# Plain float32 scores in two row halves, plain float32 diagonal products, one pool of eight banks, and new planner costs

## The chip, the core and the metric

The kernel runs on one core of a Trainium2 chip. The metric is the time of one execution in microseconds on the device. The core's engines work side by side and meet through semaphores: PE (TensorE, the matmuls; PEld is its weight load), DVE (VectorE), ACT (ScalarE), POOL (GpSimd) and SP (SyncE, which issues most DMAs). PE writes to PSUM, which has eight banks; POOL works on SBUF alone.

## The reference, cut to what matters

A gated recurrent attention (mLSTM) over 4 batches, 8 heads, 768 positions and 40 channels a head is followed by a token mix of rank 32 and an MLP from 320 to 1280 to 320 channels, all in float32.

```python
for t in range(S):                                    # attention, per batch and head
    m_new = max(f[t] + m, i[t])
    C = exp(f[t] + m - m_new) * C + exp(i[t] - m_new) * outer(v[t], k[t])
    n = exp(f[t] + m - m_new) * n + exp(i[t] - m_new) * k[t]
    m = m_new
    y[t] = sigmoid(o[t]) * (C @ q[t]) / max(abs(n @ q[t]), 1)
x  = y, heads side by side                            # [B, 768, 320]
u  = x + (x^T @ U @ V)^T                              # mix over the positions
out = u + relu(u @ w1) @ w2
```

## The kernel before

The recurrence is computed in chunks of 128 positions. Each batch has two halves (`hf`) of three chunks; in each half the heads form groups of 3, 3 and 2, so a batch has 16 units of one head and one half. For a unit:
- `scores` (line 775) multiplies k and q of each chunk on PE, 3 matmuls of 128 columns into one PSUM bank (`ps`).
- `decay_scan` (760) builds the products of the forget gates, `dm`, by a scan on DVE. Its input is a row of gates spread over 128 partitions: a PE matmul (`decay`, 757, in PSUM) for the first 11 units, a DMA (`load_decay`, 759, tile `fd` in SBUF) for the others.
- `weigh` (777) multiplies scores and decays on DVE into `wt`.
- `pv` (799) is the diagonal product of `wt` and the values on PE.

For each group come `kv` (695) and `inter` (808), the sums of keys and values for the state C and the part that the state gives; `state`, `norm`, `out_norm` and `gate` finish x.

Two precisions exist side by side. Of 64 units the first 21 multiply q and k as plain float32 with 40 rows (`SPLIT_FROM`). The others split them into a rounded part (`qk_high`, 743, a cast on ACT) and remainders (`qk_low`, 745, on POOL or DVE), stacked to 120 rows in the tile `sk`, so that one matmul in the faster float32r format makes the sum. In the same way the first 19 units multiply `wt` and v as plain float32 (`BF_FROM`, by whole groups); the others cut both into three bfloat16 parts (`thirds`, 609: `part1` and `part2` on ACT, `rest1` and `part3` on POOL or DVE) and add six products of parts, 18 matmuls a unit.

The MLP of one half (`mlp`, 914) runs 10 steps: `up` (935), 8 matmuls of 384 columns of high and low weight parts; `relu_high` (942, ACT) and `relu_low` (944, DVE); `down` (964), 9 matmuls of 320 columns. The weights arrive as 64-bit words, and 22 pieces are converted by ACT (518) and three DVE steps each (519, 521, 523) before `w_high` (567) and `w_low` (568) make the parts.

The order on every engine is made when the program is built: `Plan.schedule` (178) picks for each engine, by its costs and by due times (`pri`), the operation that can start first; the queues then run in that order. Where PE would be empty, `keep_busy` (145) puts in matmuls of zeros (`zeros`), called fillers below. `BANKS` and `SHARE` (95, 96) give three banks to `down` and five to all else. MLP steps of batch b lie among the attention of batch b + 1. The program adds its work in this order: gates, weights, attention of batch 0, then for each batch the attention of the next, two mixes and two MLPs.

Of the kernel before, what the change touches and what calls it, by code (L numbers as in the profile page):

```python
# [20 lines left out]
P = 128  # L21
# [21 lines left out]
STACK = 3 * D  # L43

PARTS = ((0, 2), (0, 1), (0, 0), (1, 1), (1, 0), (2, 0))
SPLIT_FROM = 21
FB_FROM = 11
BF_FROM = 18
# [19 lines left out]
WIDE_DMA = 630.0  # L68

# [12 lines left out]
    "qk": (3, [STACK, 2, HS], F32),  # L82
    "sk": (1, [STACK, 2, HS], F32R),
# [11 lines left out]
BANKS = {"m2": 3, "ps": 5}  # L95
SHARE = {"st": ("ps", 5), "at": ("ps", 5), "m1": ("ps", 5)}
# [5 lines left out]
class Plan:  # L102


    def __init__(self, slots):
        self.slots = {tag: [[tile, 0.0, None, tag] for tile in tiles] for tag, tiles in slots.items()}
        self.ops, self.at, self.busy = [], {}, defaultdict(float)
# [8 lines left out]
    def op(self, kind, pri, eng, cost, fn, r=(), w=(), new=(), stream="", load=1.0):  # L116
# [26 lines left out]
        self.ops.append((pri, eng, cost, fn, sorted(deps), after, new, owners, load))  # L143

# [33 lines left out]
    def schedule(self, filler, ENGINE):  # L178
# [8 lines left out]
        free, ring, dma = defaultdict(lambda: BEGIN), 0.0, 0.0  # L187
        ready = {n: 0.0 for n in range(len(ops)) if waits[n] == 0}
        left = dict(self.uses)
        while ready:  # L190
            picks = {}
            for n, est in ready.items():
                pri, engs, cost, fn, deps, after, new, owners, load = ops[n]
                s = est
                for key, tag in new:
                    group, most = SHARE.get(tag, (tag, len(self.slots.get(tag, ()))))
                    open_at = [sl[1] for sl in self.slots[group] if sl[2] is None]
                    s = max(s, min(open_at)) if open_at and self.held[tag] < most else float("inf")
                if s == float("inf"):
                    continue  # L200
                if isinstance(engs, str):
                    picks.setdefault(engs, []).append((max(s, free[engs]), pri, n))
                else:
                    done = [max(s, free[e]) + c for e, c in zip(engs, cost)]
                    e = engs[done.index(min(done))]
                    picks.setdefault(e, []).append((max(s, free[e]), pri + (ALT_PRI if e == "dve" else 0), n))
# [54 lines left out]
def mlstm_mixer_kernel(  # L261
# [91 lines left out]
    def gates():  # L353
# [29 lines left out]
        for hf in range(2):  # L383
# [11 lines left out]
            def start(hf=hf, m=m, fs=fs):  # L395
# [6 lines left out]
                "gate_max", pre, "dve", 530,  # L402
# [11 lines left out]
            def ends(bst=bst, fs=fs):  # L414
# [17 lines left out]
                "gate_w", pr, "dve", 469,  # L432
# [7 lines left out]
                "gate_g", pr, "dve", 469,  # L440
# [177 lines left out]
    def attention(b, base):  # L618
# [5 lines left out]
        def at(n):  # L624
            return base + 88.6 * n / span
# [6 lines left out]
        def group(j, n):  # L632
# [62 lines left out]
            p.op("kv", at(n - 0.5), "pe", 215 * nk, kvmm, r=[(kt, "k"), kv2], w=[kk], new=[(kk, "st")], stream="att", load=0.95)  # L695
# [33 lines left out]
            for hh in range(nh):  # L729
                bh = b * NHEAD + h0 + hh  # L730
                u = n + hh
                kqk, ksk, kdm, kw, kfb, ks = [(s, b, j, hh) for s in ("qk", "sk", "dm", "wt", "fb", "sp")]
                split = u + 16 * b >= SPLIT_FROM
                rows = STACK if split else D

                def load_qk(kqk=kqk, hh=hh, rows=rows):
                    nc.sync.dma_start(
                        out=T[kqk][0:rows].rearrange("p n s -> p (n s)"), in_=qk[b, h0 + hh, hf, 0:rows],
                    )

                p.op("load_qk", at(u) - 7, "sp", dma(rows * 2 * HS * 4), load_qk, w=[kqk], new=[(kqk, "qk")])
                if split:
                    p.op("qk_high", at(u - 1), "act", 733, lambda kqk=kqk, ksk=ksk: nc.scalar.copy(T[ksk], T[kqk]),  # L743
                         r=[kqk], w=[(ksk, 0), (ksk, 1)], new=[(ksk, "sk")])
                    for n2, lo in ((0, slice(0, D)), (1, slice(64, 64 + D))):
                        p.op("qk_low", at(u - 1), *both(HS), lambda e, n2=n2, lo=lo, kqk=kqk, ksk=ksk: e.tensor_sub(  # L746
                            T[ksk][lo, n2, :], T[kqk][lo, n2, :], f32(T[ksk][lo, n2, :])), r=[kqk], w=[(ksk, n2)])
# [8 lines left out]
                if u + 16 * b < FB_FROM:  # L756
                    p.op("decay", at(u), "pe", 165, fbmm, r=[("fhl", hf), ("fh", hf), ("idents",)], w=[kfb], new=[(kfb, "at")], load=0.5)
                else:
# [5 lines left out]
                    r=[kfb, ("idents",)], w=[kdm], new=[(kdm, "dm")],  # L764
                )

                def scmm(ks=ks, ksk=ksk, kqk=kqk, split=split):
                    for c in range(3):
                        cs = slice(c * P, (c + 1) * P)
                        if split:  # L770
                            mm(T[ks][:, cs], T[ksk][:, 1, cs], T[ksk][:, 0, cs])
                        else:
                            mm(T[ks][:, cs], T[kqk][0:D, 1, cs], T[kqk][0:D, 0, cs])

                p.op("scores", at(u), "pe", 330 if split else 640, scmm, r=[(ksk, 0), (ksk, 1)] if split else [kqk], w=[ks], new=[(ks, "at")],
                     load=0.45 if split else 0.31)
# [7 lines left out]
                def pvmm(hh=hh, kw=kw, kpb=kpb):  # L784
# [15 lines left out]
                    "pv", at(u + 1), "pe", 460 if fine else 640, pvmm,  # L800
                    r=[(k, i) for k in (kpb, kvb) for i in range(3)] if fine else [kw, (kt, "v")], w=[(kn, hh)],
                    new=[(kn, "st")] if hh == 0 else [], stream="att", load=0.65 if fine else 0.32,
# [6 lines left out]
                "inter", pf, "pe", 215 * (3 - c0), immm,  # L809
# [280 lines left out]
```

## Time and profile before

| | us |
|---|---|
| median of 3 runs | 486.63 (485.9 to 488.29) |
| span of the profiled execution | 484.6 |
| PE busy | 433.1 (89%) |
| DVE busy | 358.4 (74%) |
| POOL busy | 242.1 (50%) |
| ACT busy | 207.8 (43%) |
| mean granted TensorE clock | 0.875 |

The span is the time from the first to the last instruction; the run's time lies about 2 us over it. A busy PE is one that has a matmul in flight, at whichever clock. The granted clock is 1.0 at 2.4 GHz and 0.5 at 1.2 GHz, so a share between is a mean over both. A float32 matmul appears in the trace as two records, a float32r or bfloat16 one as one. Matmuls overlap, so the time that a block takes is read from its start to the start of the block behind it.

### The profile page before, as it was taken

Reading aid. Unit: us, or ns where it says so; the run is one execution under the profiler, and the core shown is the slowest. Engines: PE = TensorE matmul, PEld = TensorE weight load, DVE = VectorE, ACT = ScalarE, POOL = GpSimd, SP = SyncE. Lnnn points to the kernel's source line nnn. Section 1 sums busy time; section 2 is a strip of 40 time slices with the busy share of each in tenths; the row PEclk is TensorE's granted clock in tenths of the full one; section 3 lists DMA queues with packets and bytes.
Section 4 is the critical chain, followed back from the end, with each engine's and each line's share of the span. In section 5 each row is a group of like instructions: output and inputs, shape, how many; then the busy total and the mean of one; then the engine's idle time right before and its main releaser. Section 6 shows DMA issues by size and latency. Waiting matters only on the chain.

```text
span 484.6 us, 8703 instructions
## 1 busy us (share of the span) xinstructions
PE 433.1 (89%) x3175; PEld 398.1 (82%) x3175; DVE 358.4 (74%) x611; ACT 207.8 (43%) x485; POOL 242.1 (50%) x229
## 2 busy tenths in 40 slices
PE   6999999996888689889879798798888999999996
PEld 4788888985777678889768688797887889999996
DVE  6655565769999999984999998968999995322132
ACT  4411120545454655563545764544556553311120
POOL 2323244569777798730776956625768660000000
PEclk9555555579789899899989999999899999999999
DMA  8325344777475464551565656722647301010011
GB/s 247 114 87 177 94 133 137 229 201 186 134 238 171 115 177 126 157 162 48 137 169 167 167 139 170 204 81 89 182 125 180 90 3 41 1 42 0 1 42 41
DMA packets 31642, 60.58 MB, mean 125 GB/s; under 512 B 4160, under 2 KB 19776, under 8 KB 31600
## 3 DMA queue, kind: packets, MB, share of 16 engines
q1 hardware_dynamic: 31407, 59.63, 43.4%
q8 instruction: 25, 0.41, 0.4%
q10 hardware_dynamic: 192, 0.40, 0.2%
q14 instruction: 18, 0.14, 0.1%
HBM read 55.79 MB, written 4.23 MB: 124 GB/s over the span
## 4 chain that ended last, share of the span: by engine, by line
PE 51%; DVE 25%; POOL 11%; issue 9%; DMA 2%; ACT 1%; POOLq 0%; DVEq 0%; SPq 0%; ACTq 0%
PE ps L284 34%; PE m L284 17%; POOL sk L746 5%; DVE dm L762 4%; DVE cv L521 2%; DMA q<-in_q 2%; DVE C L701 2%; DVE sk L746 2%; DVE h L944 2%; DVE cv L523 2%; DVE wt L777 2%; POOL v L662 1%; POOL h L866 1%; DVE wt L612 1%; DVE pb L614 1%
## 5 line engine op out<-in xcount | busy, mean ns | idle before, releaser
L284 PE MATMUL ps<-ut,w1h 128*128 128x384 f32 x400 | 125.7, 352 | 3.6 <-DVE h L944 2.4
L284 PE MATMUL m<-w2h,h 128*128 128x320 f32 x480 | 127.6, 322 | 0.0
L746 POOL TENSOR_TENSOR sk<-qk,sk 40x384 fp32r<-40x384 f32 x62 | 85.1, 1373 | 53.0 <-ACT sk L743 14.0
L284 PEld LDWEIGHTS m<-w2h,h 128*128 128x128 f32 x480 | 87.9, 196 | 0.0
L284 PE MATMUL ps<-ut,w1l 128*128 128x384 f32 x240 | 82.7, 344 | 0.0
L284 PEld LDWEIGHTS ps<-ut,w1h 128*128 128x128 f32 x400 | 76.7, 195 | 5.3 <-DVE h L944 3.1
L944 DVE SCALAR_TENSOR_TENSOR h<-ps,h 128x384 fp32r<-128x384 f32 x80 | 43.6, 548 | 48.6 <-ACT h L942 48.2
L284 PE MATMUL m<-w2l,h 128*128 128x320 f32 x240 | 76.2, 317 | 0.0
L942 ACT ACTIVATE h<-ps 128x384 fp32r<-128x384 f32 x80 | 38.7, 487 | 70.9 <-PE ps L284 59.4
L762 DVE TENSOR_TENSOR_SCAN dm<-fd,ident 128x384 f32<-128x384 f32 x53 | 67.7, 1278 | 0.2
L777 DVE TENSOR_TENSOR wt<-ps,dm 128x384 f32<-128x384 f32 x64 | 34.8, 547 | 17.0 <-PE ps L284 16.7
L743 ACT CAST sk<-qk 120x768 fp32r<-120x768 f32 x43 | 35.8, 832 | 26.5 <-PE ps L284 23.5
L284 PEld LDWEIGHTS m<-w2l,h 128*128 128x128 f32 x240 | 47.1, 196 | 0.0
L284 PEld LDWEIGHTS ps<-ut,w1l 128*128 128x128 f32 x240 | 46.9, 195 | 0.0
L284 PE MATMUL ps<-sk 120*128 120x128 f32 x129 | 23.3, 292 | 25.0 <-DVE sk L746 12.3
L284 PEld LDWEIGHTS ps<-sk 120*128 120x128 f32 x129 | 19.6, 202 | 30.2 <-POOL sk L746 12.4
L284 PE MATMUL m<-zeros 128*128 128x256 bf16 x193 | 37.4, 340 | 1.1 <-DVE x L398 1.1
L613 ACT CAST pb<-wt 128x384 bf16<-128x384 f32 x45 | 22.9, 511 | 32.1 <-POOL wt L612 16.1
L662 POOL TENSOR_TENSOR v<-tk,tok 128x369 f32<-128x369 f32 (+1 forms) x23 | 21.1, 919 | 29.9 <-PE ps L284 21.4
L284 PE MATMUL ps<-vb,pb 128*128 128x41 bf16 x810 | 29.8, 181 | 6.8 <-DVE pb L614 4.2
L284 PEld LDWEIGHTS <-pb 128*128 128x128 bf16 x810 | 24.8, 96 | 13.1 <-DVE pb L614 5.3
L827 POOL TENSOR_TENSOR tk<-tk,rd 128x360 f32<-128x360 f32 (+1 forms) x17 | 15.6, 915 | 38.5 <-DVE rd L823 38.5
(112 smaller groups left out, 800.8 us busy)
## 6 DMA issues: line engine op xcount, KB each, us to landing
qk<-in_qk SPq DMA_DIRECT2D x43, 360.0 KB
fd<-fsd SPq DMA_DIRECT2D x53, 192.0 KB
tk<-in_tk SPq DMA_DIRECT2D x16, 544.5 KB
raw<-in_w SPq DMA_DIRECT2D x20, 320.0 KB
out<-o SPq DMA_DIRECT2D x24, 160.0 KB
tk<-in_tk SPq DMA_DIRECT2D x8, 363.0 KB
q<-in_q SPq DMA_DIRECT2D x16, 180.0 KB
qk<-in_qk SPq DMA_DIRECT2D x21, 120.0 KB
```

What stands on the lines that cost most here:

```text
L284: nc.tensor.matmul(o, a, b, start=start, stop=stop, **kw)
L521: p.op("weight_sign", pri, "dve", dve(n), lambda tu=tu, hi=hi: V.scalar_tensor_tensor(tu(), hi(), 0x80000000, tu(), ALU.bitwise_and, ALU.b ...
L523: p.op("weight_tail", pri, "dve", dve(n), lambda tu=tu, lo=lo: V.scalar_tensor_tensor(tu(), lo(), 29, tu(), ALU.logical_shift_right, ALU.b ...
L613: p.op("part2", pri, "act", act(n), lambda: nc.scalar.copy(to(1), src()), r=[ks], w=[(kd, 1)])
L662: p.op("v2", at(n - 1), ("pool", "dve"), (pool(3 * wd) * 0.83, dve(3 * wd)), lambda e: e.tensor_mul(v2v(), vtv(), tokv(1, gi, hf, DV)), r= ...
L743: p.op("qk_high", at(u - 1), "act", 733, lambda kqk=kqk, ksk=ksk: nc.scalar.copy(T[ksk], T[kqk]), r=[kqk], w=[(ksk, 0), (ksk, 1)], new=[(k ...
L746: p.op("qk_low", at(u - 1), *both(HS), lambda e, n2=n2, lo=lo, kqk=kqk, ksk=ksk: e.tensor_sub(T[ksk][lo, n2, :], T[kqk][lo, n2, :], f32(T[ ...
L762: lambda kfb=kfb, kdm=kdm: nc.vector.tensor_tensor_scan(T[kdm], T[kfb][:, 0:HS], ident3.rearrange("p c t -> p (c t)"), 0.0, ALU.mult, ALU. ...
L777: p.op("weigh", at(u), "dve", dve(HS), lambda ks=ks, kw=kw, kdm=kdm: nc.vector.tensor_mul(T[kw], T[ks][:, 0:HS], T[kdm]), r=[ks, kdm], w=[ ...
L827: p.op("out_norm", pf, ("pool", "dve"), (pool(3 * r) * 0.83, dve(3 * r)), lambda e: e.tensor_mul(otv(), otv(), rdv().unsqueeze(3).to_broad ...
L942: p.op("relu_high", pri + m - 1000, "act", 371, lambda: nc.scalar.activation(T[kh][:, 0, :], T[kp][:, 0:HS], AF.Relu), r=[kp], w=[(kh, 0)] ...
L944: p.op("relu_low", pri + m - 1000, "dve", dve(HS), lambda: nc.vector.scalar_tensor_tensor(T[kh][:, 1, :], T[kp][:, 0:HS], 0.0, f32(T[kh][: ...
```

## The change

1. `SPLIT_FROM` is gone: all 64 units multiply q and k as plain float32 with 40 rows. Two heads share one tile `qk`, one in partitions 0 to 39 and one in 64 to 103, and one operation of six matmuls takes them in turn, into two banks.
2. `BF_FROM` is 64, past every group: all 64 units take the plain product of `wt` and v. No `thirds` are left.
3. `FB_FROM` goes from 11 to 16: PE spreads the decay rows for the whole of batch 0.
4. One pool of 8 banks (`ps`), with limits of 4, 4, 3 and 3 for the four uses.
5. The planner holds an SBUF port: POOL operations and the DVE kinds in `LOCKED` don't overlap in its plan. It finds free slots for several tiles of one operation. Its costs for PE and for the gate scans are larger for most kinds (`up` 650 to 694, `down` 406 to 440 ns), and it has a price `PLAIN` of 222 ns for one plain matmul, and for one pair of score matmuls.

On PE, in the attention of batch 0: `ps<-qk` are scores, `tk,wt` diagonal products, `C,q` `inter`, `v,tk` `kv`. Before:

```order
L284 MATMUL ps_142<-C_106,q_0_100 128x123 x2
L284 MATMUL ps_140<-qk_107 128x128 x3
L284 MATMUL ps_138<-tk_96,wt_113 128x41 x3
L284 MATMUL ps_139<-v_0_99,tk_97 120x123 x3
L284 MATMUL ps_138<-tk_96,wt_114 128x41 x3
L284 MATMUL ps_138<-C_104,q_1_101 128x82
```

The same stretch now, where `fhl` is a decay row:

```order
L296 MATMUL ps_139<-v_0_99,tk_96 80x82 x2
L296 MATMUL ps_135<-qk_108 128x128
L296 MATMUL ps_138<-qk_108 128x128
L296 MATMUL ps_135<-qk_108 128x128
L296 MATMUL ps_138<-qk_108 128x128
L296 MATMUL ps_135<-qk_108 128x128
L296 MATMUL ps_138<-qk_108 128x128
L296 MATMUL ps_140<-fhl_68,idsel 128x384
L296 MATMUL ps_134<-tk_95,wt_112 128x41 x3
L296 MATMUL ps_134<-tk_95,wt_113 128x41 x3
```

Scores of two heads stand as one block that changes banks with each matmul, and the two products follow each other.

On DVE, in the attention of a middle batch beside the MLP (`h` is `relu_low`, `o` the residual, `dm` the scan, `sk`, `pb` and `tk` with `vb` the splitting). Before:

```order
L777 TENSOR_TENSOR wt_113<-ps_141,dm_111 128x384
L762 SCALAR_TENSOR_TENSOR dm_111<-fd_116,ident_64 128x384
L967 TENSOR_TENSOR o_121<-m_0_135,x_82 128x320
L944 SCALAR_TENSOR_TENSOR h_88<-ps_138,h_88 128x384
L746 TENSOR_TENSOR sk_110<-qk_109,sk_110 40x384
L612 TENSOR_TENSOR wt_113<-wt_113,pb_128 128x384
L614 TENSOR_TENSOR pb_128<-wt_113,pb_128 128x384
L612 TENSOR_TENSOR tk_96<-tk_96,vb_129 128x246
```

Now:

```order
L949 SCALAR_TENSOR_TENSOR h_87<-ps_136,h_87 128x384
L713 SCALAR_TENSOR_TENSOR C_105<-C_105,dect_71 120x123
L783 TENSOR_TENSOR wt_112<-ps_134,dm_110 128x384
L783 TENSOR_TENSOR wt_113<-ps_141,dm_111 128x384
L779 SCALAR_TENSOR_TENSOR dm_110<-fd_114,ident_64 128x384
L779 SCALAR_TENSOR_TENSOR dm_111<-fd_115,ident_64 128x384
```

Nothing stands between the scan, `weigh` and the other kinds that the MLP and the state need; two heads go through side by side.

On DVE, among the conversion of the weights (519, 521, 523, now 531, 533, 535). Before:

```order
L521 SCALAR_TENSOR_TENSOR cv_132<-raw_125,cv_132 128x320
L823 RECIPROCAL rd_120<-rd_120 128x9
L612 TENSOR_TENSOR wt_113<-wt_113,pb_128 128x384
L523 SCALAR_TENSOR_TENSOR cv_132<-raw_125,cv_132 128x320
L944 SCALAR_TENSOR_TENSOR h_88<-ps_140,h_88 128x384
L568 TENSOR_TENSOR w2l<-cv_134,w2h 128x320
```

Now:

```order
L535 SCALAR_TENSOR_TENSOR cv_132<-raw_124,cv_132 128x320
L779 SCALAR_TENSOR_TENSOR dm_110<-fd_114,ident_64 128x384
L580 TENSOR_TENSOR w2l<-cv_131,w2h 128x320
L580 TENSOR_TENSOR w2l<-cv_130,w2h 128x320
L531 TENSOR_SCALAR cv_133<-cv_133 128x320
L580 TENSOR_TENSOR w2l<-cv_132,w2h 128x320
```

DVE takes low parts of weights (580) that POOL had, and conversion pieces stand closer together.

The diff, cut to its core:

```diff
-SPLIT_FROM = 21
-FB_FROM = 11
-BF_FROM = 18
+FB_FROM = 16
+BF_FROM = 64
+PLAIN = 222.0
...
-    "qk": (3, [STACK, 2, HS], F32),
-    "sk": (1, [STACK, 2, HS], F32R),
+    "qk": (3, [P, 2, HS], F32),
...
-BANKS = {"m2": 3, "ps": 5}
-SHARE = {"st": ("ps", 5), "at": ("ps", 5), "m1": ("ps", 5)}
+BANKS = {"ps": 8}
+SHARE = {"st": ("ps", 4), "at": ("ps", 4), "m1": ("ps", 3), "m2": ("ps", 3)}
...
+        def begin(e, s, n):
+            s = max(s, free[e])
+            return max(s, port) if e == "pool" or (e == "dve" and self.lock[n]) else s
...
+                if eng == "pool" or (eng == "dve" and self.lock[n]):
+                    port = end[n]
...
-                if split:
-                    p.op("qk_high", at(u - 1), "act", 733, lambda kqk=kqk, ksk=ksk: nc.scalar.copy(T[ksk], T[kqk]),
-                         r=[kqk], w=[(ksk, 0), (ksk, 1)], new=[(ksk, "sk")])
...
+                if h % 2 == 0:
+                    pair = [("sp", b, hf, h + i) for i in range(2)]
+                    for i in range(2):
+                        def load_qk(kqk=kqk, h=h, i=i):
+                            nc.sync.dma_start(
+                                out=T[kqk][64 * i:64 * i + D].rearrange("p n s -> p (n s)"), in_=qk[b, h + i, hf, 0:D],
+                            )
...
+                    def scmm(pair=pair, kqk=kqk):
+                        for c in range(3):
+                            cs = slice(c * P, (c + 1) * P)
+                            for i, ks in enumerate(pair):
+                                rs = slice(64 * i, 64 * i + D)
+                                mm(T[ks][:, cs], T[kqk][rs, 1, cs], T[kqk][rs, 0, cs])
+
+                    p.op("scores", at(u), "pe", 3 * PLAIN, scmm, r=[(kqk, 0), (kqk, 1)], w=pair, new=[(ks, "at") for ks in pair], load=0.6)
...
-                    "pv", at(u + 1), "pe", 460 if fine else 640, pvmm,
+                    "pv", at(u + 1), "pe", 460 if fine else 3 * PLAIN, pvmm,
```

## Rows read from the trace of the kernel before

**Rows 1.** Busy us (instructions) by stretch, all engines, then granted clock, DMA share, GB/s.

```profile
core 0: us, PE busy (x) PEld busy (x) DVE busy (x) ACT busy (x) POOL busy (x), PEclk, DMA share, GB/s
...
13.00:105.00 92.00, 92.00 (x392) 78.29 (x391) 53.19 (x103) 23.08 (x67) 38.56 (x42) 0.50 0.46 143
...
116.00:167.00 51.00, 39.12 (x296) 35.33 (x297) 50.56 (x75) 25.68 (x61) 38.50 (x36) 0.89 0.56 164
167.00:394.00 227.00, 198.04 (x1778) 185.14 (x1776) 203.28 (x336) 123.06 (x282) 147.95 (x130) 0.97 0.51 138
394.00:485.00 91.00, 86.43 (x595) 85.44 (x595) 32.03 (x64) 22.17 (x48) 4.88 (x5) 0.99 0.07 23
```

**Rows 2.** PE's matmuls in time (start us, us); its decay-row group; the closing chain.

```profile
85.36 1.65 PE L284 MATMUL ps<-qk 40*128 40x128 f32 x6
86.94 1.50 PE L284 MATMUL ps<-tk,wt 128*128 128x41 f32 x6
88.24 1.56 PE L284 MATMUL ps<-v,tk 128*120 128x123 f32 x6
...
105.01 0.93 PE L284 MATMUL ps<-qk 40*128 40x128 f32 x6
105.87 0.39 PE L284 MATMUL m<-zeros 128*128 128x256 bf16 x2
...
107.47 1.38 PE L284 MATMUL m<-zeros 128*128 128x256 bf16 x11
108.68 0.76 PE L284 MATMUL ps<-tk,wt 128*128 128x41 f32 x6
109.27 0.69 PE L284 MATMUL ps<-C,q 120*128 120x123 f32 x4
109.71 0.42 PE L284 MATMUL ps<-vst,pst 128*128 128x384 f32 x1
...
115.86 0.41 PE L284 MATMUL ps<-ut,w1h 128*128 128x384 f32 x1
...
227.79 0.62 PE L284 MATMUL ps<-vb,pb 128*128 128x41 bf16 x18
228.26 0.53 PE L284 MATMUL ps<-sk 120*128 120x128 f32 x3
228.63 0.36 PE L284 MATMUL m<-w2h,h 128*128 128x320 f32 x1
...
L284 PE MATMUL ps<-fhl,idsel 64*128 64x384 f32 x10 | 6.8, 681 | 0.0
...
434.32 1.41 PE ps L284 x8
435.74 1.31 PE m L284 x9
```

**Rows 3.** Single lines of DVE: ns min/median/max, first and last start us, shapes.

```profile
L762 DVE TENSOR_TENSOR_SCAN dm<-fd,ident x53: 900/998/2573, 65.5 to 391.8; 128x384 f32<-128x384 f32 x53
L762 DVE TENSOR_TENSOR_SCAN dm<-ps,ident x11: 956/958/958, 12.9 to 64.7; 128x384 f32<-128x384 f32 x11
...
L523 DVE SCALAR_TENSOR_TENSOR cv<-raw,cv x22: 349/555/1205, 27.4 to 166.4; 128x320 uint32<-128x320 uint32 x20, 128x192 uint32<-128x192 uint32 x2
...
L944 DVE SCALAR_TENSOR_TENSOR h<-ps,h x80: 523/548/560, 121.9 to 477.5; 128x384 fp32r<-128x384 f32 x80
```

**Rows 4.** Waits of the whole span: us in total, times, longest us.

```profile
ACT pb L613 <- POOL wt L612: 16.1, 10, 2.5
...
PE ps L284 <- DVE sk L746: 12.3, 10, 2.5
```

**Rows 5.** Whole span, instructions of tile `sk`, then `pb`, then `vb` alone (columns: rows 1).

```profile
0.00:485.00 485.00, 23.32 (x129) 19.59 (x129) 21.14 (x24) 35.76 (x43) 85.15 (x62) 0.87 0.44 125
...
0.00:485.00 485.00, 29.80 (x810) 24.83 (x810) 43.41 (x60) 45.36 (x90) 32.40 (x30) 0.87 0.44 125
...
0.00:485.00 485.00, 29.80 (x810) 14.60 (x21) 15.67 (x34) 13.03 (x13) 0.87 0.44 125
```

More of the change, by code (lines that the diff above doesn't have):

```diff
@@ L114, in owner, with op @@
         return key[0] if isinstance(key[0], tuple) else key
-    def op(self, kind, pri, eng, cost, fn, r=(), w=(), new=(), stream="", load=1.0):
+    def op(self, kind, pri, eng, cost, fn, r=(), w=(), new=(), stream="", load=1.0, lock=None):
         pri += ORDER.get(kind, 0.0) + (ORDER0.get(kind, 0.0) if self.batch == 0 else 0.0)
@@ L194, in schedule @@
                 s = est
-                for key, tag in new:
+                for tag, n_new in Counter(tag for key, tag in new).items():
                     group, most = SHARE.get(tag, (tag, len(self.slots.get(tag, ()))))
-                    open_at = [sl[1] for sl in self.slots[group] if sl[2] is None]
-                    s = max(s, min(open_at)) if open_at and self.held[tag] < most else float("inf")
+                    open_at = sorted(sl[1] for sl in self.slots[group] if sl[2] is None)
+                    fits = len(open_at) >= n_new and self.held[tag] + n_new <= most
+                    s = max(s, open_at[n_new - 1]) if fits else float("inf")
                 if s == float("inf"):
@@ L729, in group @@
             for hh in range(nh):
-                bh = b * NHEAD + h0 + hh
+                h = h0 + hh
+                bh = b * NHEAD + h
                 u = n + hh
[L732 to L739, printed above, removed]
@@ L741, in group @@
-                p.op("load_qk", at(u) - 7, "sp", dma(rows * 2 * HS * 4), load_qk, w=[kqk], new=[(kqk, "qk")])
-                if split:
-                    p.op("qk_high", at(u - 1), "act", 733, lambda kqk=kqk, ksk=ksk: nc.scalar.copy(T[ksk], T[kqk]),
-                         r=[kqk], w=[(ksk, 0), (ksk, 1)], new=[(ksk, "sk")])
-                    for n2, lo in ((0, slice(0, D)), (1, slice(64, 64 + D))):
-                        p.op("qk_low", at(u - 1), *both(HS), lambda e, n2=n2, lo=lo, kqk=kqk, ksk=ksk: e.tensor_sub(
-                            T[ksk][lo, n2, :], T[kqk][lo, n2, :], f32(T[ksk][lo, n2, :])), r=[kqk], w=[(ksk, n2)])
+                kdm, kw, kfb = [(s, b, hf, h) for s in ("dm", "wt", "fb")]
@@ L756, in group @@
                 if u + 16 * b < FB_FROM:
-                    p.op("decay", at(u), "pe", 165, fbmm, r=[("fhl", hf), ("fh", hf), ("idents",)], w=[kfb], new=[(kfb, "at")], load=0.5)
+                    p.op("decay", at(u), "pe", 190, fbmm, r=[("fhl", hf), ("fh", hf), ("idents",)], w=[kfb], new=[(kfb, "at")], load=0.42)
                 else:
@@ L763, in group @@
                         T[kdm], T[kfb][:, 0:HS], ident3.rearrange("p c t -> p (c t)"), 0.0, ALU.mult, ALU.add),
-                    r=[kfb, ("idents",)], w=[kdm], new=[(kdm, "dm")],
+                    r=[kfb, ("idents",)], w=[kdm], new=[(kdm, "dm")], lock=u + 16 * b >= FB_FROM,
                 )
[L767 to L776, printed above, removed]
                 p.op("weigh", at(u), "dve", dve(HS), lambda ks=ks, kw=kw, kdm=kdm: nc.vector.tensor_mul(T[kw], T[ks][:, 0:HS], T[kdm]),
@@ L963, in down @@
                 r += [(kst, 0)] + [("vst", c) for c in range(2)]
[L964 removed]
+            p.op("down", pri + m + LAG + 0.5, "pe", 587 if m == 0 else 440, ops, r=r, w=[ka], new=[(ka, "m2")] if m == 0 else [])
             if last:
```

43 lines of the change are left out of this document (24 added, 19 removed).

## The prediction, made before the changed kernel ran

> **What bounds the kernel now.** The page's table of shares names no bound, because PE, DVE and POOL are each the busiest somewhere. So I cut the span at the events that the work itself sets (the clock's step, the first `up` matmul, the last piece of weight conversion, the last scores) and took the busy time and granted clock of each stretch [rows 1].
> - 13 to 105 us, attention of batch 0: PE never idles (92.00 of 92) at a granted clock of 0.50, so at the 1.2 GHz level; DVE works 53 of 92. PE is the bound, at half rate.
> - 105 to 116: the mix matmuls, and fillers until the first `up` at 115.86 [rows 2].
> - 116 to 167, weight conversion: DVE 50.56 of 51. The first residual of `relu` starts at 121.9, the last conversion step (L523) at 166.4 [rows 3]. DVE is the bound.
> - 167 to 394, three times the MLP of one batch beside the attention of the next: PE 198, DVE 203, POOL 148 of 227. Nobody is full, and the waits show a chain that runs through DVE and POOL: PE waits for `sk` from DVE, ACT for the remainder of `wt` from POOL [rows 4].
> - 394 to the end: MLP alone, PE 86 of 91. Its price per matmul is the cleanest of the trace: 8 `up` in 1.41 us, 9 `down` in 1.31 [rows 2], so 0.176 and 0.146 each.
>
> **What is removed.** The split of q/k and the thirds of `wt` and v disappear everywhere: DVE 21.1 + 43.4 + 14.6 = 79 us, POOL 85.2 + 32.4 + 13.0 = 131 us, ACT 35.8 + 45.4 + 15.7 = 97 us [rows 5]. On ACT nothing of it sets the end. On DVE and POOL it counts from 116 to 394. There is a second gain: scans that read two SBUF operands take 958 ns with the decay in PSUM and up to 2573 with the decay in SBUF, and the conversion step L523 349 to 1205 [rows 3], which goes with POOL working beside them; of the 219 POOL instructions in its order 99 are left.
>
> **What is added.** On PE, from full-clock rows [rows 2]: a split head's scores took 0.37 us (228.26 to 228.63) and a fine diagonal product 0.47 (227.79 to 228.26). A plain head of scores takes 0.86 (105.01 to 105.87), a plain product 0.59 (108.68 to 109.27). Products: 45 heads x 0.12 = +5 us. For scores no row shows two row halves at once. Bounds: the pair costs as much as one head (0.86), or twice that (1.72). Below one head it can't fall, as each half still streams its own three blocks of columns. Against two split heads (0.74) that is +0.1 to +1.0 us a pair. I take 0.86: the six matmuls alternate between row halves and between two PSUM banks, and the nearest row, one head alone, already shows each matmul at 0.287 us against 0.22 for the full-height `inter` ones (109.27 to 109.71 for two), so there is waiting in it that a partner could fill. The Trainium skill (TensorE: Matmul & The Clock Gate, "Part 3: Packing small matmuls — row/col tiling") says that matmuls in different row groups start about 4 ns apart and run together; by it the pair is 0.86 too, and no run here shows it. The Trainium skill (TensorEngine Tiling (Array Packing), "Key Properties") also has a rule that speaks against the change: a switch of the tiling mode drains the engine. Any such price already lies within the 0.86 - 3 x 0.22 = 0.2 us by which a lone 40-row block exceeds a full-height one, so it does not come on top.
>
> **What I cost at nothing.** The q/k loads shrink (40 rows for 120), but the DMA engines are busy 0.46 to 0.56 of the time [rows 1], so the bytes were not what the end waited for. One pool of banks can make `up`, `down` and scores wait for each other's banks; the cover is PE's queue itself, which is now the longest, and a bank that is read late costs PE about one DVE instruction of 0.55 us each time [rows 3]. A hundred of those would be 55 us; the 4% of idle PE that I leave in step 3 pay for a dozen. The planner's new port rule and costs work through the order alone, which I counted as it stands.
>
> **The sum, stretch by stretch**, against the profiled 484.6 us.
> 1. *To the first `up`.* In PE's order the matmuls ahead of it change from 21 plain heads of scores (and a split one) to 13 pairs, from 19 products to 22, from 11 decay rows to 16, and from 130 fillers to 155. At the 1.2 GHz level one head's scores take 1.58 us (85.36 to 86.94), a product 1.30 (86.94 to 88.24), a decay row 0.68; a filler takes 0.11 at full clock (11 from 107.47 to 108.68) and twice that below [rows 2]. Scores: 21 x 1.58 - 13 x 1.58 = -12.6; decay rows +3.4; products, which fall behind the clock's step, 3 x 0.6 = +1.8; fillers, 25 of which most stand in the runs of 18, 9 and 32 behind batch 0's attention, +3.5 at 0.11 to 0.22. Together -4: first `up` at 112.
> 2. *To the last conversion step.* DVE bound it, from 121.9 to 167 = 45 us (36 at the medians of its kinds: POOL was busy 38.5 of 51). Behind its first `relu` remainder DVE's order now holds 14 conversion pieces instead of 12, 8 scans instead of 5, and 10 low parts of weights instead of 1, but no thirds: 47 us at the medians, 42 at the shortest tenth. POOL keeps some 15 instructions of a microsecond there, so I take 45 again: last step at 112 + 2 + 45 = 159.
> 3. *To the last scores.* PE's queue holds from there 273 `up` x 0.176 = 48.0, 333 `down` x 0.146 = 48.6, 16 pairs x 0.86 = 13.8, 34 products x 0.6 = 20.4, 34 `kv` and 33 `inter` x 0.22 = 14.7, and 14 us of mixing, transposes and 20 fillers: 160 us. DVE has 116 to 130 us there, POOL under 50. The same sum for before is 186 us in 227, or 82%. With DVE at about 75% and no split chain I take 96%: 167 us, so 326.
> 4. *To the end.* 121 us by the same prices, 3 more for the last residual and store: 124. Span 450. The median of the runs lies 2.0 over the span: **452 us**, 34.6 less than 486.63.
>
> At 100% of PE in step 3, and a pair at the price of three full-height matmuls (0.66), this is 441; at 88%, 467.
>
> **The rivals.**
> - *The halves do not run together* (the change doesn't do what it says). Then a pair costs 1.3 (six matmuls at 0.22) to 1.72: before the first `up` 13 x (1.1 to 1.6) at half rate, after the conversion 16 x (0.4 to 0.86): +21 to +34, so 473 to 486; say 477. For it: no row shows concurrency. Against it: separate rows, separate banks, and alternating order.
> - *The first stretch runs at the full clock.* Rows show PE without a pause and still at half rate for 92 us [rows 1]; it is at full rate again at 105, behind mixing matmuls, `kv` and fillers. If paired scores and the run of nine fillers do that near 15 us, batch 0's attention is through PE near 60 us and DVE bounds the start with its 71 to 80 us ahead of the first `relu` remainder: first `up` near 86 instead of 112, so 426. The Trainium skill (TensorE: Matmul & The Clock Gate, "Part 1: The HAM clock gate") has the rule that activity lifts the throttle, and would have it so; the row of 92.00 in 92 at 0.50 disagrees with its plain reading.
> - *Slower: the low level spreads to every attention stretch.* What batch 0 shows at 0.50 is scores, products and `kv` in plain float32. The change makes the attention of batches 1 to 3 of the same matmuls, where bf16 products and stacked scores stood. If PE drops to 1.2 GHz whenever they come, the 49 us of scores, products, `kv` and `inter` in step 3 take 98, with neighbouring `up`: 452 + 49 = 501. From a loss of 36 us on it is slower than before, so from about three quarters of those matmuls at the low level. Against it: 0.97 in 167 to 394, and long runs of `up` and `down` between them in the new order.
> - *Another wait takes the place of `sk`.* PE stops for `weigh` of both heads, DVE being in order behind `relu` remainders: step 3 stays at 82%, 195 us instead of 167: 480. For it, the waits of today [rows 4]; against it, DVE has a third less to do.
>
> **How the numbers follow.** Forecast 0.60; halves serial 0.15; full clock early 0.10; step 3 no denser 0.08; low level spread 0.07. The range for 8 in 10 runs from 427 (the early clock) to 479 (most of the serial case, and the waits). About 0.5% (2.4 us) is what a measurement can tell from no change, so same means 484.2 to 489.1. Serial halves and waits at their worst end there: same 0.03; slower, from the spread of the low level, 0.07; faster 0.90.
>
> **What would show it.** Right: a pair of score blocks start to start at 0.65 to 0.9 us at full clock; half clock until 90 to 97 us, first `up` near 112; L523's counterpart ending near 159 with DVE full; PE over 93% from there; POOL near 85 us in all. Wrong: pairs at 1.3 or more; a clock of 1.0 before 60 us; granted clock below 0.9 after 167; `weigh` named as releaser of PE for more than 15 us.

## The result, and the profile after

The changed kernel (called after in what follows) takes 458.27 us (median of 4 runs, 454.78 to 459.19); the kernel before (called before) took 487.06 beside it. The ratio is 0.9485, with a 95% interval from 0.9343 to 0.9628. The forecast was 452.0. The profiled execution has a span of 456.6 us against 484.6, so 28.0 us are gone.

First the stretches, cut at the same events as [rows 1]: first `up`, last conversion step, last scores. Columns are the time, the busy us of each engine, the granted clock, the DMA share and GB/s.

```profile
core 0: us, PE busy (x) PEld busy (x) DVE busy (x) ACT busy (x) POOL busy (x), PEclk, DMA share, GB/s
13.00:107.00 94.00, 93.62 (x525) 79.87 (x524) 56.95 (x121) 27.77 (x82) 33.45 (x38) 0.57 0.49 148
107.00:154.00 47.00, 39.43 (x289) 35.86 (x289) 42.50 (x93) 21.01 (x51) 10.82 (x11) 0.96 0.65 192
154.00:333.00 179.00, 167.33 (x1201) 160.36 (x1200) 108.07 (x226) 43.48 (x118) 34.57 (x37) 0.95 0.41 116
333.00:457.00 124.00, 120.21 (x770) 119.75 (x768) 38.62 (x80) 26.34 (x56) 1.89 (x3) 0.99 0.05 17
```

In [rows 1] the stretch behind the conversion was full on no engine (PE 198, DVE 203, POOL 148 of 227). Now PE works 167.33 of 179, DVE 108.07, POOL 34.57: PE is the bound from there to the end. In the first stretch PE was and is the bound, mostly at half rate: the clock's record has the 1.2 GHz level from 11.6 to 93.5 us in one piece, and later again for 3.4, 3.4 and 13.7 us (from 137.8, 226.6 and 267.5), 20.5 us in all until the last scores. The record of before has it for 92.2 us ahead of the first `up`, and for 27.4 us behind it, in seven pieces.

Four moments in PE's timeline of after: two pairs of heads at the low level, the second with a decay row behind it, the first `up`, and a pair at the full clock.

```profile
14.40 1.65 PE L296 MATMUL ps<-qk 40*128 40x128 f32 x12
15.98 0.40 PE L296 MATMUL ps<-zeros 128*128 128x256 bf16 x1
...
27.40 1.65 PE L296 MATMUL ps<-qk 40*128 40x128 f32 x12
28.70 0.98 PE L296 MATMUL ps<-fhl,idsel 64*128 64x384 f32 x2
...
107.42 0.42 PE L296 MATMUL ps<-ut,w1h 128*128 128x384 f32 x1
...
181.63 0.94 PE L296 MATMUL ps<-qk 40*128 40x128 f32 x12
182.50 0.44 PE L296 MATMUL ps<-ut,w1h 128*128 128x384 f32 x1
```

A pair takes 182.50 - 181.63 = 0.87 us, what one head took in [rows 2] (0.86). At the low level it takes 1.58. In four of the nine cases there the next block starts 1.30 behind the pair's start; in all four that block is a decay row of 64 rows, which starts while the pair still runs (the pair from 27.40 lasts 1.65, the row starts at 28.70), so 1.30 is not the price of a pair.

DVE's single lines answer to [rows 3]: ns min/median/max, first and last start.

```profile
L779 DVE TENSOR_TENSOR_SCAN dm<-fd,ident x48: 898/948/2304, 74.1 to 334.8; 128x384 f32<-128x384 f32 x48
...
L779 DVE TENSOR_TENSOR_SCAN dm<-ps,ident x16: 929/956/958, 13.7 to 72.6; 128x384 f32<-128x384 f32 x16
...
L535 DVE SCALAR_TENSOR_TENSOR cv<-raw,cv x22: 346/484/1153, 36.5 to 151.9; 128x320 uint32<-128x320 uint32 x20, 128x192 uint32<-128x192 uint32 x2
...
L949 DVE SCALAR_TENSOR_TENSOR h<-ps,h x80: 499/557/560, 109.6 to 449.8; 128x384 fp32r<-128x384 f32 x80
```

Scans with the decay in SBUF have a median of 948 ns (998 before) and a mean of 1033 (1278 before), and a few still take up to 2304. What PE waits for between 154 and 333 us (total, times, longest) is little and scattered; the `sk` of [rows 4] is gone, and `weigh` (L783) did not take its place:

```profile
PE ps L296 <- DVE h L949: 3.8, 2, 2.9
PE ps L296 <- DVE x L838: 2.9, 2, 1.8
PE ps L296 <- DVE wt L783: 2.7, 2, 2.4
PE ps L296 <- DVE h L872: 1.3, 1, 1.3
```

### The profile page after: what moved, and what is told of

Its sections match the earlier page's. It is cut to its first block, busy times and chain, and to the rows that moved or that the text cites. A ratio compares the mean times of both kernels' runs of the same rounds, so it can differ in the third digit from the quotient of the medians.

```text
span 456.6 us, 7500 instructions
## 1 busy us (share of the span) xinstructions
PE 430.2 (94%) x2839; PEld 402.9 (88%) x2839; DVE 254.4 (56%) x534; ACT 123.7 (27%) x317; POOL 82.6 (18%) x96
## 4 chain that ended last, share of the span: by engine, by line
PE 74%; DMA 13%; DVE 9%; issue 2%; ACT 1%; SPq 1%; DVEq 0%; ACTq 0%
PE ps L296 73%; DMA fd<-fsd 6%; DMA tk<-in_tk 4%; DVE dm L779 3%; DMA qk<-in_qk 2%; DMA raw<-in_w 1%; DVE cv L535 1%; DVE cv L533 1%; DVE wt L783 1%; DMA q<-in_q 1%; DVE h L949 1%; DVE cv L531 0%; DVE C L713 0%; DVE o L972 0%; PE ps L466 0%
## 5 line engine op out<-in xcount | busy, mean ns | idle before, releaser
L296 PE MATMUL ps<-w2h,h 128*128 128x320 f32 x480 | 121.6, 314 | 0.0
L949 DVE SCALAR_TENSOR_TENSOR h<-ps,h 128x384 fp32r<-128x384 f32 x80 | 43.8, 554 | 92.2 <-ACT h L947 91.8
L296 PEld LDWEIGHTS ps<-w2h,h 128*128 128x128 f32 x480 | 84.5, 190 | 0.5
L296 PE MATMUL ps<-w2l,h 128*128 128x320 f32 x240 | 74.4, 310 | 1.0 <-DVE w2l L580 1.0
L296 PEld LDWEIGHTS ps<-tk,wt 128*128 128x128 f32 x384 | 62.0, 239 | 7.1 <-issue 4.6
L296 PE MATMUL ps<-tk,wt 128*128 128x41 f32 x384 | 62.8, 318 | 3.8 <-DVE wt L783 3.1
L779 DVE TENSOR_TENSOR_SCAN dm<-fd,ident 128x384 f32<-128x384 f32 x48 | 49.0, 1033 | 7.5 <-DMA fd<-fsd 7.5
L296 PE MATMUL ps<-zeros 128*128 128x256 bf16 x263 | 43.4, 314 | 8.7 <-DVE wt L783 4.7
L296 PEld LDWEIGHTS ps<-w2l,h 128*128 128x128 f32 x240 | 45.5, 190 | 1.3 <-DVE w2l L580 1.3
L296 PEld LDWEIGHTS <-zeros 128*128 128x128 bf16 x263 | 27.9, 113 | 18.7 <-issue 10.7
L296 PE MATMUL ps<-qk 40*128 40x128 f32 x384 | 38.6, 342 | 2.2 <-DMA qk<-in_qk 2.2
L783 DVE TENSOR_TENSOR wt<-ps,dm 128x384 f32<-128x384 f32 x64 | 33.8, 543 | 7.9 <-PE ps L296 7.7
L296 PEld LDWEIGHTS ps<-qk 40*128 40x128 f32 x384 | 31.4, 234 | 7.7 <-DMA qk<-in_qk 2.8
```

What stands on the lines that cost most here:

```text
L296: nc.tensor.matmul(o, a, b, start=start, stop=stop, **kw)
L779: lambda kfb=kfb, kdm=kdm: nc.vector.tensor_tensor_scan(T[kdm], T[kfb][:, 0:HS], ident3.rearrange("p c t -> p (c t)"), 0.0, ALU.mult, ALU. ...
L783: p.op("weigh", at(u), "dve", dve(HS), lambda ks=ks, kw=kw, kdm=kdm: nc.vector.tensor_mul(T[kw], T[ks][:, 0:HS], T[kdm]), r=[ks, kdm], w=[ ...
L949: p.op("relu_low", pri + m - 1000, "dve", dve(HS), lambda: nc.vector.scalar_tensor_tensor(T[kh][:, 1, :], T[kp][:, 0:HS], 0.0, f32(T[kh][: ...
```

## The experiments

Executions of one kernel differ by the clock that PE was granted, so the table gives the range of each kernel's mean granted clock, and time times clock for every run. That product estimates what the run would take with the clock always full; it is exact only where PE is the bound. In f2_old_work_back it hardly moves (450.01 us at 0.945 and 466.29 at 0.908, products 425.3 and 423.4), but in e5_qk5 it grows with the clock, from 400.9 at 0.879 to 411.8 at 0.913. So a difference of up to 10 between the products of two kernels says little when their clocks differ, and after was seen at 0.879 to 0.886 alone.

| kernel | median us | runs | granted clock | time x clock, median (range) |
|---|---|---|---|---|
| before, beside the experiments | 486.8 | 33 | 0.864 to 0.893 | 425.5 (422.9 to 429.6) |
| after | 458.3 | 4 | 0.879 to 0.886 | 403.6 (399.8 to 406.1) |
| e1_by_head | 464.1 | 4 | 0.878 to 0.895 | 408.2 (407.8 to 412.1) |
| e2_plain_old_plan | 514.6 | 4 | 0.867 to 0.895 | 450.3 (446.6 to 453.1) |
| e3_no_port | 446.2 | 4 | 0.888 to 0.918 | 401.5 (396.5 to 407.9) |
| e4_burst | 447.8 | 4 | 0.898 to 0.934 | 409.9 (407.9 to 412.9) |
| e5_qk5 | 452.4 | 4 | 0.879 to 0.913 | 404.0 (400.9 to 411.8) |
| e6_thirds_back | 457.7 | 4 | 0.894 to 0.942 | 412.1 (410.9 to 416.3) |
| e7_no_port_burst | 448.3 | 4 | 0.887 to 0.912 | 407.1 (402.4 to 409.2) |
| e8_splits_back | 452.0 | 4 | 0.901 to 0.916 | 410.3 (408.2 to 413.1) |
| f1_one_pool_only | 482.8 | 10 | 0.882 to 0.890 | 428.7 (426.5 to 431.2) |
| f2_old_work_back | 463.2 | 4 | 0.908 to 0.945 | 423.0 (422.6 to 425.3) |
| f5_splits_no_port | 464.5 | 4 | 0.883 to 0.911 | 417.1 (414.4 to 420.4) |
| g1_plain_one_pool | 490.8 | 10 | 0.826 to 0.868 | 413.8 (410.3 to 419.5) |

### Do the row halves run together?

e1_by_head computes the same, with the six matmuls head by head instead of in turn:

```diff
-for c in range(3):
-    for i, ks in enumerate(pair):
+for i, ks in enumerate(pair):
+    for c in range(3):
```

> The changed kernel, but the six score matmuls of a pair run head by head (three in the lower row half, then three in the upper) instead of in turn. Every queue but PE's own score blocks is unchanged. Theory (the two row halves run side by side because neighbours in the queue lie in different halves): a pair grows from 0.87 us at full clock to 1.4 to 1.7, and from 1.3-1.58 to 2.4-3 at half clock; 13 pairs ahead of the first up matmul and 16 behind the conversion give 475 to 490 us. Rival 1 (halves run side by side whatever the order, or scores are hidden): 458 within 3. Rival 2 (a pair is one head long because a weight load hides, not because halves overlap): pair about 1.3, 468 to 475.

```profile
37.05 2.24 PE L296 MATMUL ps<-qk 40*128 40x128 f32 x12
39.22 0.43 PE L296 MATMUL ps<-tk,wt 128*128 128x41 f32 x1
...
185.78 1.26 PE L296 MATMUL ps<-qk 40*128 40x128 f32 x12
186.97 0.44 PE L296 MATMUL ps<-ut,w1h 128*128 128x384 f32 x1
```

In its timeline a pair takes 1.19 us at the full clock and 2.17 at the low one, against 0.87 and 1.58. All three expectations missed: theory and rival 2 had the pair and the total too long, rival 1 too short; rival 2's pair of 1.3 is nearest. Six full-height matmuls, at the 0.22 us that [rows 2] give for one, would take 1.3. In turn the six take 0.87, which is well below that, so there the halves do run together; head by head they take 1.19, not far below it, so rival 2 (in turn, waiting is hidden) may be a part of the difference, and no run separates the two. In turn is worth some 6 us at equal clock: three runs of e1 take 463.67 to 465.69 at 0.878 to 0.885, the fourth 456.25 at 0.895, and after 454.78 to 459.19 at 0.879 to 0.886. The Trainium skill (TensorE: Matmul & The Clock Gate, "Part 3: Packing small matmuls — row/col tiling") has matmuls in different row groups run side by side. The 0.87 for two heads agrees with it; the 1.19 shows that the order of issue decides how much of it one gets.

### Is the removed work the gain?

e2_plain_old_plan makes the kernel before plain, in its own planner and banks:

```diff
-SPLIT_FROM = 21
+SPLIT_FROM = 64
-BF_FROM = 18
+BF_FROM = 64
-SHARE = {"st": ("ps", 5), ...}
+SHARE = {"st": ("ps", 4), ...}
```

> The kernel before with its planner, costs and order rules, only that all heads take plain float32 scores (one head at a time in the lower rows) and plain diagonal products; one limit of the shared banks falls from 5 to 4 so that a plan exists. No pairs, no port rule, no new costs. Theory (the gain comes from the work taken off DVE and POOL, a part of it from pairs): the first 116 us stay, the conversion stretch gets shorter by some us, and the middle needs 18 + 5 us more of PE at a higher density: 465 to 482. Rival (the planner and the pairs made all of the gain; plain float32 costs what it frees): 487 or more.

It took 514.63 us, 30 more than the kernel before beside it. The theory failed and the number lies in the rival's range; PE's timeline shows where: the first `up` starts at 189.63.

```profile
189.38 0.55 PE L284 MATMUL m<-zeros 128*128 128x256 bf16 x3
189.63 0.62 PE L284 MATMUL ps<-ut,w1h 128*128 128x384 f32 x1
```

The conversion of the weights was over at 151; plain heads need no preparation by DVE or POOL, and the old planner put 39 heads of scores ahead of the first `up` (21 plain ones and a split one before), and 282 fillers for 130. Less work is no gain while the order does not let the MLP begin.

g1_plain_one_pool adds to that kernel only the pool of 8 banks with after's limits, without pairs, new costs or port rule:

```diff
-BANKS = {"m2": 3, "ps": 5}
-SHARE = {"st": ("ps", 4), "at": ("ps", 5), "m1": ("ps", 5)}
+BANKS = {"ps": 8}
+SHARE = {"st": ("ps", 4), "at": ("ps", 4), "m1": ("ps", 3), "m2": ("ps", 3)}
```

> The kernel before, all heads plain and no thirds, single heads instead of pairs, the old costs and no port rule, but the one pool of 8 banks. The same without the pool took 514.6, with the first up at 190 us; in the order of this one 25 heads of scores stand ahead of the first up, not 39, so first up at 115 to 128. Theory: the pool is what makes plain scores usable, and the pairs are worth 11 x 1.6 us at half clock and some 11 x 0.86 at full: 470 to 480. Rival: without pairs and the new costs the old order's trouble stays: 495 or more.

The first `up` is at 116.9, as expected, and the product falls from 450.3 to 413.8. But the time, 490.78, is no gain on the kernel before (ratio 1.0018, 0.996 to 1.0075) and 11 over the expected range: of all kernels this one had the lowest clock (0.826 to 0.868). So the removal of the work and the pool do not make the gain without the rest, which is pairs, decay rows, the port rule and the new costs; only the port rule is undone by itself, in e3, and no run undoes the costs.

f1_one_pool_only makes the same edit of the banks alone in the kernel before, with its splits and thirds.

> The kernel before with one edit: one pool of 8 banks, with after's limits on each use, in place of 3 banks for down and 5 for the rest. Splits, thirds, costs and single heads stay. My theory since the thirds and the splits could come back at no cost: the split chain was bound by the order and by the banks, and the gain behind the conversion comes from the one pool; then it takes 462 to 474. Rival: the pool alone moves nothing while DVE and POOL still hold the split work: 482 to 490.

482.85 us: the rival held, the pool alone gains nothing. The row behind the conversion answers to the third of [rows 1] and is the same within a few us (DVE 204.04 of 228, POOL 152.83).

```profile
165.00:393.00 228.00, 199.22 (x1827) 185.20 (x1826) 204.04 (x342) 125.83 (x289) 152.83 (x132) 0.99 0.51 138
```

Now the reverse: after, with the removed work put back. e6_thirds_back cuts `wt` and v into thirds again:

```diff
-BF_FROM = 64
+BF_FROM = 18
```

> The changed kernel, but wt and v are again cut into bf16 thirds from step 18 on (plan, pairs and the banks as after). Theory: the thirds cost more by their work on POOL, DVE and ACT (20 to 25 us of DVE, 85 of POOL, 60 of ACT after the first up) and by DVE's scans slowed beside POOL than the 5 us they save on PE, so the stretch with the MLP of one batch beside the attention of the next gets 8 to 20 us longer: total 466 to 478. Rival: with PE the bound after the conversion the other engines have room for the thirds, and the cheaper products count: total 453 to 457. Rival two: the removal of the thirds was nearly the whole gain: 478 or more.

e8_splits_back splits q/k again from step 22 on:

```diff
+if u + 16 * b >= 22:      # one head: load 120 rows, qk_high, qk_low, one stacked product
+    ...
-if h % 2 == 0:
+elif h % 2 == 0:
```

> The changed kernel, but from step 22 on a head's q/k is again split into stacked high and low parts and its scores are one stacked product (no pairs there; 4 tiles for q/k, no tiles for thirds). Theory: 2 us less on PE, but 17 us more on DVE, up to 43 on POOL and 35 on ACT, and the chain q/k load, high part, low part, scores is back: total 463 to 475. Rival: with room on DVE and POOL since the thirds went, nothing of it stands on the path: 455 to 459.

f2_old_work_back has both edits, with 3 tiles for q/k as in after.

> The changed kernel (its planner, its pool of banks, paired scores up to step 21) with both removed parts back: stacked scores from step 22, thirds from step 18. The theory of the prediction, that the work taken off DVE and POOL is what gives the time back, says 470 to 485. The theory that it is the order and the pool says 452 to 464, as with each of the two parts alone.

The theory of the prediction missed in all three. e6 took 457.67 us, next to its first rival, and e8 452.0, below its own, so by time each part alone comes back at no cost. f2 took 463.16 (450.01 to 466.29), which is inside the range for order and pool and outside 470 to 485; its quickest run, at a clock of 0.945, is below all four of after. So the time, as it stands, does not say that the removed work is the gain.

The clock stands in between. In the product thirds back cost +8.5, splits back +6.7 and both +19.4, of the 425.5 - 403.6 = 21.9 that the change is worth, but these three kernels ran at higher clocks than after, so the numbers are too high. At equal clock f2 (462.38 at 0.914, 463.93 at 0.911, 466.29 at 0.908) lies some 11 to 16 us over e5 of the next part, which has after's work (451.04 at 0.913, 449.65 at 0.903). A third estimate takes the traces behind the first `up` and counts time at 1.2 GHz as half: 338 us for after, 337 for e8, 344 for e6 and 353 for f2. By these two estimates both parts cost 11 to 16 us, and one alone 0 to 6: neither alone gives it back, because the room that one leaves on DVE is enough for the other. Ahead of the first `up` hardly anything of the gain is the removed work: it starts at 106.72 in f2 and 107.42 in after, at 115.86 in before. The rows behind the conversion show where the old work goes, e8, e6 and f2 in turn (of f2 the conversion too):

```profile
158.00:362.00 204.00, 194.36 (x1326) 186.87 (x1324) 164.58 (x324) 80.52 (x174) 28.17 (x28) 0.99 0.56 148
```

```profile
163.00:356.00 193.00, 182.60 (x1776) 171.10 (x1775) 158.20 (x316) 86.83 (x214) 53.83 (x56) 0.98 0.38 111
```

```profile
107.00:156.00 49.00, 44.62 (x381) 41.29 (x380) 48.01 (x101) 27.02 (x65) 15.64 (x15) 1.00 0.51 147
156.00:378.00 222.00, 211.15 (x2015) 199.76 (x2015) 214.32 (x417) 127.60 (x284) 63.20 (x63) 1.00 0.53 148
```

With one part back PE stays the bound (194.36 of 204, 182.60 of 193) and DVE is at about 80%. With both, DVE works 214.32 of 222 and is the bound. (The old work comes back mostly on DVE, 356.4 us in all for 254.4, and little on POOL, 113.7 for 82.6, which had 242.1 in before.) PE looks full too, but some 22 of its 211 us there are fillers (194 of them). And the clock is 1.00: f2, with 534 fillers in all, does not fall to 1.2 GHz from 91 us until its last microsecond, where after does for 20.5 us. So **against f2 the changed kernel gave back in granted clock most of what it had gained in work**, and takes only 4.9 us less; before, with 27.4 us at 1.2 GHz behind its first `up`, had no such clock. That the fillers hold the clock is argued from this one kernel; no run changed them alone in that stretch, and other counts of fillers do not order the clock cleanly (e4 below has 299 in all, after 263, and e4 is at the low level for 44 us behind its first `up`).

### Do late loads cost the changed kernel its 12 us of idle PE?

The chain of waits of after runs through loads between 225 and 250 us (`tk` 5.83 and 4.88 us, `fd` 5.62), and between 154 and 333 us SP waits 30.6 us for tiles of q/k to come free, with other loads queued behind. e5_qk5 gives q/k five tiles:

```diff
-    "qk": (3, [P, 2, HS], F32),
+    "qk": (5, [P, 2, HS], F32),
```

> The changed kernel with 5 tiles for q/k instead of 3 (the unused tiles of the thirds make the room). My theory for the 17 us that the stretch between the last conversion step and the last scores is longer than forecast: part of it is loads that come late, because a q/k load that waits on SP for its tile holds up the loads behind it. Then that stretch falls from 184 us to 176 to 181 and the total to 450 to 456. Rival: the late loads only stand where PE would have waited anyway, and the lost time there is the two or three drops of the clock alone: 184 us stays, total 457 to 460.

```profile
13.00:97.00 84.00, 79.31 (x529) 68.54 (x529) 59.10 (x124) 28.22 (x81) 33.02 (x38) 0.72 0.59 176
...
144.00:325.00 181.00, 168.52 (x1194) 161.75 (x1194) 107.56 (x224) 43.33 (x118) 34.23 (x37) 0.93 0.39 112
```

The time fell into the range of my theory, but the stretch did not get shorter: 181 us for 179, PE idle 12.5 for 11.7. SP still waits 29.3 us for q/k. So the loads are not shown to cost anything, and the rival holds for that stretch. What got shorter is the first stretch, to which the next part belongs.

### The clock of the first stretch

PE's order in e5 is, instruction for instruction, that of after, and so are DVE's and ACT's; only some early loads on SP and one instruction on POOL moved. Yet the clock rises at 19 us in e5 and not in after (page, granted clock in 40 slices, after and then e5):

```profile
PEclk9555555599998999999999976999999999999999
```

```profile
PEclk9697555989989979999699969999999999999999
```

The same matmuls in both timelines, again after and then e5 (`kv` ends, a decay row, two products, a decay row):

```profile
19.99 0.68 PE L296 MATMUL ps<-fhl,idsel 64*128 64x384 f32 x1
20.60 2.78 PE L296 MATMUL ps<-tk,wt 128*128 128x41 f32 x12
23.31 0.69 PE L296 MATMUL ps<-fhl,idsel 64*128 64x384 f32 x1
```

```profile
19.21 0.43 PE L294 MATMUL ps<-fhl,idsel 64*128 64x384 f32 x1
19.57 1.53 PE L294 MATMUL ps<-tk,wt 128*128 128x41 f32 x12
21.04 0.44 PE L294 MATMUL ps<-fhl,idsel 64*128 64x384 f32 x1
```

Two products take 2.71 us in one and 1.47 in the other. e5 has 47.8 us at the low level before its first `up`, after 81.9, and the first `up` comes at 96.5 instead of 107.4. Its four runs part the same way: 449.65 and 451.04 at a clock of 0.903 and 0.913, 453.72 and 456.09 at 0.886 and 0.879. The Trainium skill (TensorE: Matmul & The Clock Gate, "Part 1: The HAM clock gate") says that the moment of the rise differs between runs of one kernel. These runs agree, and between these two traces it is worth 11 us. What decides it is not shown: one trace of each kernel was kept, and e5's own runs differ as much.

e4_burst puts a run of fillers on PE near 16 us, to lift the clock on purpose:

```diff
+if s > 13000.0 and not self.burst:
+    self.burst = True
+    for _ in range(36):
+        filler(s)
```

> The changed kernel with 36 more filler matmuls in one run on PE near 16 us, nothing else moved on any queue. Theory (PE at the 1.2 GHz level bounds 12 to 94 us, and a dense run lifts it as the runs near 94 us did): the fillers cost 4 to 8 us, the granted clock is 1.0 soon behind them and mostly stays, the first up comes near 85 to 95 us instead of 107, total 435 to 450. Rival 1 (the level falls back with the first scores and products behind the run): 462 to 466. Rival 2 (DVE or loads bound the first stretch as soon as PE is faster): first up still above 100, total 452 to 460.

447.82 us, ratio to before 0.9203 (0.9091 to 0.9316), first `up` at 94.5: both lie where the theory put them. The clock is at the low level for 41.0 us ahead of the first `up` instead of 81.9. But that the fillers lift it is not shown. In the clock's record it rises at 18.8 us, and their run has only begun:

```profile
18.35 4.35 PE L301 MATMUL ps<-zeros 128*128 128x256 bf16 x36
22.62 0.43 PE L301 MATMUL ps<-fhl,idsel 64*128 64x384 f32 x1
```

In e5 it rises at 19.1 without such a run, and in after, at 93.5, it rises ahead of the runs of 18 and 9 fillers (94.91 and 97.86). Nor does it stay: e4 is at the low level again from 29.1 to 42.7 and from 59.8 to 80.3. What e4 and e5 do show is that the first stretch hangs on the level: 41 us less of it bring the first `up` 12.9 us forward in e4, 34 us less bring 10.9 in e5.

e3_no_port takes the port rule out of the planner:

```diff
-if eng == "pool" or (eng == "dve" and self.lock[n]):
-    port = end[n]
```

> The changed kernel without the planner's port rule: POOL and DVE operations may overlap in the plan, so operations go back to POOL and the order on all engines changes. Arithmetic unchanged. Theory (the rule acts through the order alone, and PE is the longest queue behind the conversion): 452 to 466. Rival (the port rule is what makes the gain, by keeping scans and conversion steps from being blocked by POOL): 472 or more, with scans of 1.2 us on the mean again.

446.19 us (444.35 to 451.43), ratio 0.9295 (0.9187 to 0.9403), the lowest median of all: below the ranges of theory and rival, and the scans with the decay in SBUF take 1.06 us on the mean, not 1.2. A part of it is the clock: the product is 401.5 for 403.6. At about equal clock it is still the faster, by 2 to 12 us: 446.55 at 0.888 and 451.43 at 0.890, against 453.72 (e5) and 458.37 (after) at 0.886. Its windows are the first three of its stretches:

```profile
13.00:96.00 83.00, 73.55 (x467) 62.07 (x468) 57.98 (x112) 29.29 (x85) 41.76 (x48) 0.70 0.58 167
96.00:135.00 39.00, 32.41 (x196) 29.02 (x195) 39.00 (x73) 15.66 (x40) 21.50 (x22) 0.91 0.58 171
135.00:319.00 184.00, 170.13 (x1246) 162.34 (x1246) 112.91 (x214) 44.58 (x118) 54.74 (x58) 0.96 0.43 125
```

POOL shares the conversion again, which takes 39 us for 47; the stretch behind it is 5 us longer; and the start is 11 us shorter at 0.70 for 0.57, so mostly by the clock (11 pairs stand ahead of the first `up` there, not 13). A planner that keeps DVE and POOL apart has not paid here.

e7_no_port_burst has both edits.

> The changed kernel without the planner's port rule and with 36 fillers in one run on PE near 16 us, the two edits that each made the start shorter. Theory: both act on the same thing, the time that PE spends at the 1.2 GHz level in the attention of batch 0, so they overlap: first up at 86 to 93, total 436 to 445. Rival: the gain without the port rule is from a better order of DVE and POOL and adds to that of the clock: total 434 or less. Rival two: the burst delays the start by its own 8 us and the clock falls again: 446 to 452.

448.32 us, first `up` at 99.4: later than the theory said, and the total lies in the range of rival two. The clock fell again at 43 us, as it does at 42 in e3 without the burst; ahead of the first `up` the low level lasts 53.1 us, for 51.2 in e3. So the burst bought no clock there and cost its own time. f5_splits_no_port is e8 without the port rule, meant as a better version.

> A version that may beat both: the changed kernel without the port rule, with stacked scores from step 22 (4 tiles for q/k, no tiles for thirds). The start without the port rule took 96 us to the first up, and the stretch from there to the end with stacked scores 337 us against 343 without the port rule. If the two add up: 433 to 442. Rival: without the port rule DVE and POOL get in each other's way once the splits need them: 446 to 455.

464.52 us: the two do not add up, and the time is over the rival's range too. Without the rule POOL works 97 us behind the conversion instead of 28, the scans with the decay in SBUF take 1.15 us on the mean instead of 1.04, and the product is 417.1 for 410.3. That DVE and POOL get in each other's way is argued from that and not shown as the cause: f5 is also at 1.2 GHz for 34 us behind its first `up`, e8 for 7.

## Why the prediction was right, and where it was off

**The reason held, for a part of the gain.** With that work removed PE is the bound behind the conversion (167.33 of 179 us), with the old work put back DVE is (f2, 214.32 of 222). What that is worth is 11 to 16 us by the two estimates that allow for the clock, 19.4 by the product, of the 28.0 gone from the span. 8.4 of the 28.0 lie ahead of the first `up`, where the pairs and the order gain them, as step 1 had it. How the rest is shared among pool, pairs, order and clock is not shown. A condition was missing from my reasoning: that the planner would use it. I counted the order as it stood, so the number was safe, but e2 shows the same removal at 514.63 with the old banks and costs.

**The price of a pair** was taken at 0.86 between 0.86 and 1.72, and is 0.87. The rival of serial halves is dead, with a remark: head by head it would have been 1.19.

**Step 1**, first `up` at 112, came at 107.4. Of its terms, read from start to start over PE's queue up to there, scores gave -12.3 (forecast -12.6), decay rows +2.5 (+3.4), products +2.7 (+1.8). The term that failed is the fillers: 25 more of them, but 27.2 us in all for 29.7 with the idle time behind them, so -2.5 and not +3.5. The fillers themselves take 0.8 us more; the idle time that they stand beside fell from 5.3 us to 2.0, and the prediction had no term for it.

**Step 2** was 45 us from the first remainder of `relu` to the last conversion step; it runs from 109.6 to 153.0 (the last step starts at 151.9 and is the longest, 1.15), so 43. DVE was busy 42.50 of 47, not full.

**Step 3** is the step that was mis-sized: 167 us forecast, 179.4 measured (153.0 to 332.4). PE's demand was right: 167.33 us busy less the 8.5 that 17.1 us at half rate cost is 159, for 160. The clock was taken as full, which is 8.5 of the 12.4; PE idles 11.7 us for 6.7, which is 5.0; the demand gives 1 back. Of that idle time 10.7 are the four waits shown above, and e5 says that they are not for want of q/k tiles. **Step 4** was 124 and is 124.

So the span is 456.6 for 450: 6.0 won up to the end of the last conversion step (153.0 for 159), 12.4 lost from there to the last scores, 0.2 in step 4. The two errors have opposite signs, so that the total came within 6.3 us of the forecast is in part luck.

**The rivals.** The early clock did not come in after (0.57 up to the first `up`), and did come for a part of the stretch with the same order of PE in e5: it was a better rival than 0.10, though what it brought there was 11 us of the first `up` and not the 26 that the prediction gave it. The low level did not spread: 20.5 us behind the first `up`, for 27.4 in before; the stretch stays at 0.95. A new wait in place of `sk` did not come: `weigh` holds PE for 2.7 us there. POOL has 82.6 us in all, for 85.

## What to carry to other kernels

When PE is the bound, look at time and granted clock together: a kernel with less work can lose in clock what it gains in work (after against f2), and an edit that seems free (e6) may have been paid for by the clock. A product of time and clock helps, but compare it between runs at about the same clock. Undo the parts of a change singly and together, since two parts that each cost little may share the same spare room. And removing work helps only if what sets the order uses the room: look first at where the next stage begins.

## What the hardware showed that was not expected

- One and the same order of PE, DVE and ACT ran the first stretch with 81.9 us at 1.2 GHz in after and 47.8 in e5. In the program only some early loads and one POOL instruction differ; e5's own runs lie between clocks of 0.879 and 0.913.
- PE stayed at 1.2 GHz for 81.9 us while it was busy 81.00 of the 81 us from 13 to 94, with 40-row scores, products of 41 columns, `kv`, `inter` and fillers (after).
- A pair in two row halves costs 0.87 us in turn and 1.19 head by head at the full clock; at half clock 1.58 in turn and 2.17 head by head, so less than twice.
